# The first q load in float32 on SyncE's queue, and another emission order at the start

## The chip, the cores and the metric

The kernel runs on one NeuronCore of a Trainium2 chip. The metric is the device time of one execution in microseconds; times are medians over several executions. The core has five engines that each work through their own list of instructions strictly in order: TensorE (PE, matmuls into PSUM), VectorE (DVE), ScalarE (ACT), GpSimd (POOL) and SyncE (SP, which here only issues transfers). An instruction starts when those before it on its engine are issued and the results and buffers it needs are there. Transfers from HBM run on 16 shared DMA engines and are issued here from SyncE's list or from GpSimd's; a transfer that also converts float32 to float16 is issued from GpSimd's list in this kernel.

## The reference

First an attention with a feature map, with q, k and v of 8 batches, 8 heads, 576 positions and 64 channels, in float32:

```python
def phi(x):
    return np.where(x > 0, x, np.exp(x) - 1.0) + 1.0
q_p, k_p = (phi(q), phi(k))
kv = np.einsum('bhsd,bhse->bhde', k_p, v)
z = np.sum(k_p, axis=2)
num = np.einsum('bhsd,bhde->bhse', q_p, kv)
den = np.einsum('bhsd,bhd->bhs', q_p, z)[..., None] + 1e-06
return (num / den).astype(np.float32)
```

Its output is taken as x with 4608 rows (positions) and 512 columns. Then comes a mixture of 8 experts: `logits = x @ w_gate`, eight Sinkhorn rounds that scale the rows and columns of exp(logits) to a matrix P (4608 x 8), and

```python
for e in range(E):
    h = np.maximum(x @ w1[e], 0.0)
    ye = h @ w2[e]
    out += P[:, e:e + 1] * ye
```

with w1 of 512 x 1024 and w2 of 1024 x 512 for each expert.

## The kernel before, in words

**The attention.** It is done in 16 groups, n = 0 to 15, n = 2b + g for batch b and half g; a group is four heads. k0, q0, v0 below are the loads of group 0, and so on. A group takes these steps; what stands in square brackets is the group:

- three loads (line 376): k into a buffer `kin` in float32, q into `qin` and v into `vv` in float16, converted on the way. k of groups 0 and 1 is issued from SyncE, all else from GpSimd. There are three buffers of each kind.
- phi(k): exp on ScalarE (L387), add and max on VectorE (L391), min on VectorE (L395). phi(q) likewise: L450, L453, L457.
- kv[n]: 18 matmuls (L416) of phi(k) with v and with ones into the one PSUM buffer `kv_ps`; two copies (L335 or L337, `kvz`) take it to SBUF.
- qt[n]: nine transposes of phi(q) (L442) into `att`, and a copy of that to `qpT` (L335 or L337).
- den[n], two halves: a pair of matmuls each (L473 into `att`), then the logarithm on ScalarE (L486); after both halves exp of its negative (L491).
- num[n], two halves: a pair of matmuls each (L473 into `num_ps`, the same PSUM buffer as kv), then on VectorE the product with the reciprocal into xT (L501).

**What else runs in that time.** 46 matmuls on a constant tile (L593, `warm`) whose result nobody reads; the weights of expert 0 (L310, from GpSimd); the logits for two batches at a time (L518, L522); the first layer of expert 0 (L687, its relu L692 or L694) and its second layer (L935) for the first blocks of 512 positions, as soon as their part of xT is there; from the fifth block on a scheme with seven products in place of eight for a 2 x 2 block product (L813 for the first layer, L1053 for the second, with sums on VectorE in L985, L1024 and L851). The Sinkhorn rounds run on VectorE with one small matmul each (L559) and end before expert 1 needs P.

**What sets the order.** The kernel builds a list of tasks (`_Plan`), each with the engine or engines it can run on, durations and dependencies, and then emits them one by one. `_FRONT` is a long string that fixes the order of the first tasks: each word is a task number and a letter for the engine (p TensorE, a ScalarE, d VectorE, g GpSimd, s SyncE, m a landing, n none). So `66d` puts task 66 (the qpT copy of group 0) on VectorE and `66a` on ScalarE. As engines work in order, the string fixes what stands behind what. After the string a planner places the rest from the tasks' durations, and from the last block of expert 0 on TensorE's order is tied into a fixed chain. In the string 2p to 47p are the warm matmuls, 65p is qt[0], 58p kv[0], 67p and 69p den[0], 86p kv[1].

GpSimd issues at most eight of its loads ahead of landings (`p_sw`), and a load into a buffer waits for the last reader of what was in it.

Of the kernel before, what the change touches and what calls it, by code (L numbers as in the profile page):

```python
# [17 lines left out]
class _Plan:  # L18
# [121 lines left out]
    1n 108n 113n 595n 76s 77m 48s 49m 2p 3p 0g 4p 50g 51m 5p 6p 78g 79m 7p 8p 52g 53m 9p 80g 81m 10p 82a 83d 11p 118g  # L140
    119m 12p 13p 14p 15p 120g 121m 16p 84d 17p 54a 18p 146g 147m 19p 55d 20p 21p 22p 122g 123m 23p 56d 24p 61n 62a
    25p 26p 63d 27p 28p 29p 64d 30p 89n 109g 110m 90a 31p 32p 91d 65p 66d 57n 58p 148g 149m 92d 33p 59a 34p 85n 150g
    151m 35p 60a 36p 37p 67p 86p 68a 38p 125d 69p 39p 40p 87d 111g 112m 131n 124a 70a 41p 88d 71a 126d 93p 42p 94d
    74p 174g 175m 152a 75d 95p 43p 44p 96a 178g 179m 45p 72p 132a 73d 127n 97p 46p 47p 133d 128p 98a 134d 99a 129d
    135p 176g 177m 130d 202g 203m 153d 136a 100p 596p 101d 114g 115m 159n 597p 137p 154d 598p 138a 102p 161d 204g
    205m 160a 155n 103d 139p 599p 156p 140a 162d 141a 157d 163p 206g 207m 600p 164d 158a 602p 232g 233m 601d 165p
    142p 166a 181d 234g 235m 604p 606p 180a 143d 608p 603d 116g 117m 144p 609a 182d 167p 610p 607a 145d 183n 187n
    236g 237m 168a 612p 189d 188a 605d 184p 611d 260g 261m 169a 190d 614p 185d 191p 186a 632n 172p 192d 106g 107m
    618p 173d 193p 209d 170p 215n 208a 613a 615a 262g 263m 194a 616p 171d 216a 195p 210d 633p 290g 291m 217d 196a
    211n 218d 212p 197a 104g 105m 634d 219p 213d 635p 220d 214a 245n 238a 264g 265m 200p 239d 221p 637p 247d 636a  # L150
    201d 222a 639p 240d 246a 292g 293m 198p 223p 199d 617p 638a 248d 640a 241n 320g 321m 242p 224a 624d 225a 619p
    243d 318g 319m 244d 249p 267d 228p 250d 620p 273n 266a 346g 347m 229d 251p 621p 268d 252a 294g 295m 274a 226p
    297d 322g 323m 253p 641p 275d 254a 276d 643p 626a 269n 227d 255a 230p 642d 303n 305d 270p 231a 304a 644d 277p
    271d 622p 272a 278d 296a 258p 306d 279p 645p 324a 374g 375m 259d 331n 325d 647p 350g 351m 280a 298d 348g 349m
    646a 256p 623p 332a 257d 404g 405m 299n 281p 326d 665n 376g 377m 300p 282a 630d 283a 333d 307p 378g 379m 301d
    651p 308d 302a 628a 284p 309p 648a 285d 666p 310a 334d 286p 311p 667d 327n 668p 312a 353d 352a 670p 287d 335p
    669d 380a 359n 491g 492m 328p 336d 653p 329a 381d 408g 409m 330a 354d 313a 406g 407m 288p 382d 432g 433m 387n
    314p 289a 654p 360a 315d 337p 661d 316p 338a 672p 355n 317d 671a 339p 361d 673a 356p 362d 434g 435m 340a 553d
    649p 388a 495g 496m 554d 674p 357d 389d 358a 341a 363p 390d 676p 364d 417n 418a 344p 419d 365p 345d 650p 366a
    420d 342p 410a 367p 343d 383n 652p 368a 411d 384p 675a 412d 460g 461m 438a 391p 385d 436g 437m 677d 678p 445n  # L160
    386a 462g 463m 392d 369a 680p 503g 679d 493g 494m 659a 372p 447d 393p 373d 699p 394a 560d 681a 370p 395p 469s
    371d 413n 655p 396a 657d 397a 414p 439d 561d 421p 415a 464g 465m 440d 416a 682p 470s 497a 422d 400p 656p 401d
    446a 508n 423p 663d 698n 398p 424a 701p 441n 399d 425p 448d 442p 426a 471s 700d 500s 427a 449p 443d 501s 562d
    684p 502s 476n 450d 444a 563s 564m 509a 428p 451p 429d 685p 452a 498d 703p 477a 478d 555d 453p 430p 499d 556s
    557m 454a 683p 565s 566m 479d 692a 504n 402p 455a 431d 558s 559m 688p 510d 704a 511d 456p 403a 466a 689p 457d
    512p 467d 702a 458p 513d 705p 459d 480p 706a 468d 505p 481d 472n 707p 506a 581d 507a 582d 514p 473p 583d 515a
    584s 585m 690a 516p 474d 709p 517a 475d 686p 518a 735d 736d 482p 687p 710a 708d 696a 519p 737d 483a 711p 520d
    484p 738d 712a 713p 485a 574d 521p 739n 740p 486a 567d 522d 721p 714a 575d 694a 489p 576d 722p 490d 577s 578m
    719p 729d 568d 487p 717p 488d 718p 569d 551n 731d 570s 571m 742p 579s 580m 732d 778d 523p 743a 572s 573m 836d
    741a 720p 725a 733d 524a 552p 727a 525n 526d 744p 746p 745a 748p 747a 837d 588g 589n 592n 838d 527p 750p 779d  # L170
    749a 780d 734d 752p 781s 782m 751a 783s 784m 528d 754p 529d 753a 715p 839s 840m 755a 841s 842m 786p 716p 787a
    586s 587m 590g 591m 756d 530p 800p 785n 757d 792p 1009s 1010m 531d 788p 532d 762p 789a 723a 794p 793a 790p 760p
    791a 801a 796p 795d 802p 761a 758d 533p 806p 803a 797d 804p 807a 759d 766p 534d 798p 535d 808p 799a 810p 805a
    764p 767a 763a 844p 770p 845a 811d 765a 809d 768p 771d 536p 850p 537d 812p 769d 851a 772p 813a 894d 848p 814d
    773a 843n 858p 849a 895d 818p 815d 860p 816d 819a 846p 859a 817d 824p 847a 896d 861a 538d 864p 897s 898m 593g
    594m 820p 865a 825a 854p 868p 862p 866p 855d 863a 852p 869d 828p 867d 870p 821d 856p 829d 826p 857a 853d 539p
    902p 540d 822p 903a 541d 908p 823a 830p 871a 906p 831a 901n 904p 909a 952d 916p 905a 918p 872d 907a 876p 873d
    919a 912p 827d 877a 910p 917a 874d 924p 882p 953d 911d 922p 1001d 542p 878p 923a 954d 883d 955s 956m 920p 879a
    957s 958m 913d 926p 921a 875d 886p 925d 899s 900m 914p 543d 884p 927d 915a 1066s 1067m 887d 880p 544d 960p 888p
    961a 928p 889a 959n 966p 929a 964p 885d 967a 545p 934p 965a 930d 881a 970p 1002d 974p 935a 546d 976p 931d 975a  # L180
    962p 932d 978p 963a 980p 547d 977a 938p 981a 982p 940p 936p 933d 941a 971d 984p 937a 944p 1003d 979a 983d 942p
    945d 968p 985d 972p 969d 986p 973a 946p 943d 1522n 987a 1004d 548p 1012p 1000n 1011n 947d 1014p 1013a 549d 990p
    1015a 550d 1018p 1020p 1019a 1016p 774a 1022p 988p 777a 1023d 951a 631d 989p 1017a 1024p 726a 996d 1026p 625d
    1028p 1027a 1021d 991p 1029a 1005d 1025a 992p 1006d 629a 993p 1007d 1008d 1032p 1034p 627d 1033a 1030p 997d 1036p
    1031a 1069p 1037d 658a 994p 834d 1070a 1035d 1071p 939a 1038p 1072a 995p 1123s 1124m 998a 1039a 1075p 1068n 1525n
    1077p 999a 1040d 1073p 1076a 1044p 1041d 1042d 1046p 1045a 1043d 1049p 1048d 1047d 1079p 1050a 1054p 1074a 1080d
    835a 1057p 1056d 1052a 776d 1081p 1053g 1059d 1083p 1055d 1085p 1084a 1058d 1060p 660d 1086a 1082a 1089p 1062d
    1091p 1078d 1090a 1087p 695d 1093p 1088a 1061d 1126p 1094d 1128p 1127a 1092d 1063p 1129a 1095p 1065d 1125n 1132p
    1064d 1096a 1180s 1181m 1523g 1524m 1051g 1134p 664d 1133a 1130p 1097d 1101p 1098d 1103p 1099d 1102a 833a 1100d
    1106p 1104d 1136p 1105d 1107a 1111p 1109a 1137d 1131a 697d 1114p 662a 730d 1112d 693a 1138p 1110g 1113d 1140p  # L190
    691a 724d 1108g 1142p 1135d 1141a 1117p 1143a 892d 1116d 1139a 1146p 1115d 1148p 1147a 1118d 1144p 1149d 1150p
    1145a 1183p 1119d 1185p 775d 1184a 1120p 1151d 1186a 1152p 1122d 1182n 1189p 1121d 1153a 1237s 1238m 1191p 1190a
    1154d 1187p 1158p 1155d 1160p 1156d 1159a 1188a 1163p 1161d 1157d 1193p 1164a 1162d 1168p 1194d 1165g 1171p 1192d
    1526g 1527m 1170d 1195p 1169d 1197p 832d 1196a 1199p 891d 1198a 1174p 1173d 1200a 1203p 1176d 1205p 1175d 1204a
    1201p 1172d 1207p 1202a 1240p 1208d 1242p 1241a 1206d 1177p 1243a 1166a 1209p 1178d 1239n 1167g 1246p 1179d 1210a
    1294s 1295m 1248p 1211d 1244p 1215p 1212d 1217p 1213d 1216a 1247a 1220p 1218d 1214d 1250p 1223a 1219d 1225p 1245a
    1251d 1228p 728d 1226d 1224g 1227d 1252p 1229d 1254p 1253a 1528d 1256p 1255a 1231p 1249d 1257a 948d 1260p 1232d
# [22 lines left out]
def kernel(  # L220
# [27 lines left out]
    S_ = _Plan()  # L248
# [109 lines left out]
    def att(b, g):  # L358
        n = 2 * b + g
        pr = n - 100.0  # L360

        src = [[NJ * D, P], [4 * S * D, 2], [1, NJ * D]]
        gin, tin = {}, {}
        for nm, ten in (("k", k), ("q", q), ("v", v)):
            gr = gin[nm] = S_.grp(p_in[nm])
            sp = nm == "k" and b == 0

            def fn(_, gr=gr, nm=nm, ten=ten, sp=sp):
# [843 lines left out]
```

## Time and profile before

| | us |
|---|---|
| median of 3 runs | 962.06 (961.62 to 962.55) |
| the profiled execution | 961.32 |
| its span, first to last instruction | 959.4 |
| TensorE busy | 949.8 |
| VectorE busy | 786.9 |
| ScalarE busy | 575.9 |
| GpSimd busy | 145.3 |

The profile shows one execution. Busy times are sums over an engine's instructions without overlap; matmuls are pipelined and their ends are modelled, so TensorE's waits are better read from the starts of neighbouring matmul groups. In the rows that follow, a line of the order in time gives the start, the duration, engine, source line, operation, output and inputs, the shape, how many were merged (x18), and in square brackets the idle time before it with what ended it. A row of the waits gives who waited for whom, the total in us, how often, and the longest. A row of the table by stretches gives, for each engine, busy time and number of instructions in that stretch, then the granted TensorE clock, the share of the DMA engines, and GB/s. The granted clock was 0.999 of full speed.

### The profile page before, as it was taken

Reading aid. Unit: us, or ns where it says so; the run is one execution under the profiler, and the core shown is the slowest. Engines: PE = TensorE matmul, PEld = TensorE weight load, DVE = VectorE, ACT = ScalarE, POOL = GpSimd, SP = SyncE. Lnnn points to the kernel's source line nnn. Section 1 sums busy time; section 2 is a strip of 40 time slices with the busy share of each in tenths; the row PEclk is TensorE's granted clock in tenths of the full one; section 3 lists DMA queues with packets and bytes.
Section 4 is the critical chain, followed back from the end, with each engine's and each line's share of the span. In section 5 each row is a group of like instructions: output and inputs, shape, how many; then the busy total and the mean of one; then the engine's idle time right before and its main releaser. Section 6 shows DMA issues by size and latency. Waiting matters only on the chain.

```text
span 959.4 us, 21109 instructions
## 1 busy us (share of the span) xinstructions
PE 949.8 (99%) x8576; PEld 804.8 (84%) x8576; DVE 786.9 (82%) x1508; ACT 575.9 (60%) x1025; POOL 145.3 (15%) x209
## 2 busy tenths in 40 slices
PE   8999999999999999999999999999999999999998
PEld 4555578788888888888888888888888888888886
DVE  6999999898888888878887888878887888877775
ACT  6999665665555555555555555555555555555552
POOL 6432000011112111211112110111112111111110
PEclk9999999999999999999999999999999999999999
DMA  9997493044225422452227222272226322235554
GB/s 229 267 246 160 153 221 116 14 111 120 78 78 131 113 78 78 119 124 78 78 78 165 79 78 78 85 158 78 73 70 130 100 71 76 75 100 165 166 165 111
DMA packets 45821, 112.52 MB, mean 117 GB/s; under 512 B 4380, under 2 KB 25628, under 8 KB 45724
## 3 DMA queue, kind: packets, MB, share of 16 engines
q1 hardware_dynamic: 21340, 76.16, 23.9%
q0 software_dynamic: 23984, 34.48, 19.2%
q8 instruction: 67, 1.10, 0.5%
q10 hardware_dynamic: 400, 0.52, 0.2%
q14 instruction: 30, 0.25, 0.1%
HBM read 119.69 MB, written 17.69 MB: 143 GB/s over the span
## 4 chain that ended last, share of the span: by engine, by line
PE 93%; DVE 3%; ACT 1%; DMA 1%; issue 1%; POOL 0%; DVEq 0%; ACTq 0%; POOLq 0%
PE ye L1053 36%; PE hq L813 24%; PE R L813 12%; PE Zye L813 6%; PE Zye L1053 6%; PE ye L935 3%; PE hq L687 2%; DMA vv<-in_v_dram 1%; PE kv_ps L416 1%; PE att L473 1%; PE att L442 1%; PE num_ps L473 1%; DVE xT L501 1%; DVE h L694 0%; ACT rden L486 0%
## 5 line engine op out<-in xcount | busy, mean ns | idle before, releaser
L1084 DVE SCALAR_TENSOR_TENSOR acc<-ye,P_sb,acc 128x256 f32<-128x256 f32 x620 | 267.9, 479 | 119.6 <-PE ye L1053 118.5
L813 PEld LDWEIGHTS <-W 128*128 128x128 f16 x2144 | 209.7, 98 | 25.3 <-issue 0.2
L1053 PEld LDWEIGHTS <-S 128*128 128x128 f16 x1984 | 194.1, 98 | 22.9 <-issue 0.4
L1094 POOL TENSOR_TENSOR acc<-acc,st 128x256 f32<-128x256 f32 x124 | 88.6, 733 | 691.2 <-ACT st L1091 677.6
L1053 PE MATMUL ye<-T,S 128*128 128x256 f16 x1488 | 192.8, 273 | 0.2 <-DVE acc L1084 0.2
L813 PEld LDWEIGHTS <-w 128*128 128x128 f16 x1608 | 157.3, 98 | 19.2 <-issue 0.5
L1053 PEld LDWEIGHTS <-h 128*128 128x128 f16 x1584 | 155.0, 98 | 17.9
L848 ACT ACTIVATE h<-hq 128x512 f16<-128x512 f32 x134 | 80.0, 598 | 142.2 <-PE hq L813 137.3
L813 PE MATMUL hq<-xs,W 128*128 128x256 f16 x1008 | 151.2, 273 | 0.0
L813 PE MATMUL R<-xs,W 128*128 128x256 f16 x1008 | 151.2, 273 | 0.0
L813 PE MATMUL hq<-xs,w 128*128 128x256 f16 x1008 | 140.9, 273 | 0.3 <-DVE h L851 0.3
L845 ACT ACTIVATE h<-Zye 128x512 f16<-128x512 f32 x134 | 80.0, 597 | 39.3 <-PE Zye L813 39.3
L1091 ACT ACTIVATE st<-Zye,P_sb 128x256 f32<-128x256 f32 x124 | 52.5, 470 | 75.4 <-PE Zye L1053 75.4
L1024 DVE TENSOR_TENSOR S<-h 128x1024 f16<-128x1024 f16 x124 | 85.4, 689 | 12.2 <-ACT h L848 12.0
L835 ACT COPY s<-hq 128x512 f32<-128x512 f32 x126 | 73.5, 583 | 36.5 <-PE hq L813 36.2
L851 DVE CUSTOM_DVE_ANT_0 h<-R,s 128x512 f16<-128x512 f32 x126 | 86.6, 687 | 9.9 <-ACT s L835 9.4
L828 ACT COPY Zye<-hq 128x512 f32<-128x512 f32 x134 | 77.7, 580 | 27.5 <-PE hq L813 27.3
L851 DVE CUSTOM_DVE_ANT_0 h<-hq,s 128x512 f16<-128x512 f32 x126 | 86.7, 688 | 6.3 <-PE hq L813 6.2
L813 PE MATMUL Zye<-xs,w 128*128 128x256 f16 x504 | 75.6, 273 | 0.0
L842 ACT COPY s<-R 128x512 f32<-128x512 f32 x126 | 74.5, 591 | 0.0
L1053 PE MATMUL ye<-w,h 128*128 128x256 f16 x528 | 68.4, 273 | 0.0
L1053 PE MATMUL Zye<-w,h 128*128 128x256 f16 x528 | 68.4, 273 | 0.0
(116 smaller groups left out, 975.4 us busy)
## 6 DMA issues: line engine op xcount, KB each, us to landing
xs<-xd SPq DMA_DIRECT2D x63, 896.0 KB, 4.6
out_dram<-acc SPq DMA_DIRECT2D x67, 128.0 KB, 2.4
w<-in_moe_w_dram POOLq DMA_DIRECT2D x16, 512.0 KB, 8.6
kin<-in_k_dram POOLq DMA_DIRECT2D x14, 576.0 KB, 9.5
w<-in_moe_w_dram POOLq DMA_DIRECT2D x7, 1024.0 KB, 13.6
qin<-in_q_dram POOLq DMA_DIRECT2D x16, 288.0 KB, 8.2
vv<-in_v_dram POOLq DMA_DIRECT2D x16, 288.0 KB, 8.7
xd<-acc SPq DMA_DIRECT2D x5, 512.0 KB, 2.9
```

Source lines behind the costliest of these rows:

```text
L813: nc.tensor.matmul(dst[:, p, :], lhsT=lhs(p, c), rhs=rhs(c), start=(first and p == 0 and c == 0), stop=(c == 1), skip_group_check=True)
L828: nc.scalar.copy(out=Zt[1], in_=gX["tile"])
L835: nc.scalar.copy(out=gs2["tile"], in_=gX["tile"])
L842: nc.scalar.copy(out=gs5["tile"], in_=gR["tile"])
L845: nc.scalar.activation(out=hd(0, 0), in_=Zt[1], func=AF.Relu)
L848: nc.scalar.activation(out=hd(1, 0), in_=gX["tile"], func=AF.Relu)
L851: nc.vector._custom_dve(TENSOR_ADD_SAT, out=dst, in0=ps, in1=sb, s0=3.0e38, s1=0.0)
L1024: nc.vector.tensor_tensor(out=Sx[:, i], in0=a0, in1=a1, op=op)
L1053: nc.tensor.matmul(bank(g_)[:, s, :], lhsT=lhs(s, kk), rhs=rhs(kk), start=(new and s == 0 and kk == 0), stop=(kk == 3), skip_group_check=True)
L1084: nc.vector.scalar_tensor_tensor(out=dst(), in0=bank(g_)[:, s, :], scalar=P_sb[:, gg, e:e + 1], in1=dst(), op0=ALU.mult, op1=ALU.add)
L1091: nc.scalar.mul(out=gst["tile"], in_=bank(g_)[:, s, :], mul=P_sb[:, gg, e:e + 1])
L1094: nc.gpsimd.tensor_tensor(out=dst(), in0=dst(), in1=gst["tile"], op=ALU.add)
```

## The change

Three things change.

First, q of group 0 is loaded in float32, from SyncE's list, into a buffer of the k kind (`kin`). SyncE's list begins with k0, q0, k1 instead of k0, k1; GpSimd's list has one load less. The exp (L450) and add-and-max (L453) of group 0 read float32; the task's duration in the plan goes from 0.455 to 0.77.

Second, the plan's earliest landing time for a load from GpSimd goes from 4.0 to 5.2.

Third, `_FRONT` is another string: 1510 words instead of 1582. GpSimd's loads then begin v0, q1, v1, k2, q2, v2, k3, two pieces of w1, q3, v3 instead of q0, q1, v0, v1, k2, q2, k3, v2, two pieces of w1, q3, v3. TensorE's list begins, with w for warm matmuls:

- before: 31 w, qt[0], kv[0], 5 w, den[0], kv[1], w, den[0], 3 w, qt[1], w, num[0], den[1], 3 w, num[0], den[1], 2 w, kv[2], qt[2], num[1], 2 half-jobs of L687, den[2], one more, num[1], den[2], one more, kv[3]
- after: 27 w, qt[0], w, kv[0], w, den[0], kv[1], den[0], 3 w, qt[1], w, num[0], 3 w, den[1], num[0], 2 w, den[1], 2 w, kv[2], 2 w, qt[2], w, num[1], 3 w, den[2], one half-job of L687, num[1], two more, den[2], kv[3]

The choice between VectorE and ScalarE for copies, relus and scalings changes with the string. The lines of the changed kernel stand one to three lower than before.

```diff
 _FRONT = """
-    1n 108n 113n 595n 76s 77m 48s 49m 2p 3p 0g 4p 50g 51m 5p 6p 78g 79m 7p 8p 52g 53m 9p 80g 81m 10p 82a 83d 11p 118g
-    119m 12p 13p 14p 15p 120g 121m 16p 84d 17p 54a 18p 146g 147m 19p 55d 20p 21p 22p 122g 123m 23p 56d 24p 61n 62a
...
+    1n 108n 113n 595n 48s 49m 50s 51m 2p 3p 76s 77m 0g 4p 52g 53m 5p 6p 78g 79m 7p 8p 80g 81m 9p 10p 55d 11p 12p 13p
+    14p 15p 16p 17p 61n 54a 118g 119m 62a 63d 18p 19p 120g 121m 20p 21p 22p 23p 122g 123m 64d 24p 25p 26p 146g 147m
...
         for nm, ten in (("k", k), ("q", q), ("v", v)):
-            gr = gin[nm] = S_.grp(p_in[nm])
-            sp = nm == "k" and b == 0
-
-            def fn(_, gr=gr, nm=nm, ten=ten, sp=sp):
+            wide = nm == "k" or n == 0 and nm == "q"
+            gr = gin[nm] = S_.grp(p_in["k" if wide else nm])
+            sp = wide and b == 0
+
+            def fn(_, gr=gr, nm=nm, ten=ten, sp=sp, wide=wide):
...
-                elif nm == "k":
+                elif wide:
                     dst = gr["tile"] = fp.tile([P, 2, NJ, D], FP32, tag="kin", name="kin", bufs=NK)
...
-            tin[nm] = fadd(("dma", 1.47 if nm == "k" else 1.42), lambda _: None, deps=[ti], use=[gr, *gsw], prio=pr, lat=2.2,
-                           after=0.0 if sp else 4.0)
+            tin[nm] = fadd(("dma", 1.47 if wide else 1.42), lambda _: None, deps=[ti], use=[gr, *gsw], prio=pr, lat=2.2,
+                           after=0.0 if sp else 5.2)
...
-        t3 = fadd(("dve", 0.455), f_qm, deps=[t0], use=[gin["q"], gtq], prio=pr)
+        t3 = fadd(("dve", 0.455 if n else 0.77), f_qm, deps=[t0], use=[gin["q"], gtq], prio=pr)
```

## The prediction

> **What bounds the kernel now.** I read the table of stretches first, then the waits and the order in time at the start.
>
> ```profile
> core 0: us, PE busy (x) PEld busy (x) DVE busy (x) ACT busy (x) POOL busy (x), PEclk, DMA share, GB/s
> 0.00:10.00 10.00, 8.67 (x31) 3.45 (x31) 5.66 (x11) 4.77 (x4) 8.29 (x17) 1.00 0.87 199
> 10.00:20.00 10.00, 8.20 (x82) 4.94 (x81) 6.73 (x11) 7.73 (x10) 4.84 (x7) 1.00 1.14 268
> 20.00:30.00 10.00, 9.28 (x87) 5.50 (x86) 9.23 (x17) 8.74 (x11) 5.77 (x9) 1.00 1.16 247
> 30.00:60.00 30.00, 29.56 (x277) 17.30 (x276) 28.67 (x48) 28.26 (x38) 13.34 (x19) 1.00 1.15 259
> 60.00:120.00 60.00, 59.42 (x543) 34.34 (x544) 57.20 (x104) 49.86 (x73) 10.31 (x17) 1.00 0.70 173
> ...
> 200.00:900.00 700.00, 699.75 (x6411) 627.00 (x6410) 567.32 (x1094) 398.51 (x749) 93.39 (x131) 1.00 0.35 99
> ```
>
> From 200 to 900 us TensorE is never free (699.75 of 700), and the change touches nothing there. Before, TensorE is still the fullest engine, but VectorE and ScalarE are nearly as full (28.67 and 28.26 of 30), and the DMA engines are full until 60 us (shares above 1). Both kernels give TensorE the same 8576 matmuls, the 46 warm ones of L593 among them. So **the time can change only by TensorE's waits**, and nearly all of those lie before 180 us.
>
> ```profile
> PE att L442 <- DVE tq L457: 1.0, 2, 0.7
> PE att L473 <- DVE qpT L337: 0.5, 1, 0.5
> PE att L442 <- ACT rden L486: 0.4, 1, 0.4
> ```
>
> These rows (first 30 us) are too small, because the modelled ends of matmuls overlap. I count from start to start instead: four 512-column matmuls take 0.865 us where nothing waits, a pair of L473 0.245, a kv group 0.85, the nine transposes 0.505, a warm one 0.216. What is above that is wait. By this count TensorE waits 4.1 us from the end of the 31st warm matmul (10.0) to the fourth kv group (25.61), 4.0 us from there to 118 us in some 22 pieces of 0.1 to 0.5, and 0.7 us between 118 and 180. More than these 8.8 us is not to be had.
>
> ```profile
> 4.81 1.16 ACT L387 ACTIVATE ek<-kin 128x1152 f16<-128x1152 f32 x1 [2.79 <-DMA kin<-in_k_dram]
> 6.26 1.16 ACT L387 ACTIVATE ek<-kin 128x1152 f16<-128x1152 f32 x1 [0.29 <-DMA kin<-in_k_dram]
> 8.83 1.16 ACT L450 ACTIVATE eq<-qin 128x1152 f16<-128x1152 f16 x1 [1.40 <-DMA qin<-in_q_dram]
> 10.39 1.16 ACT L450 ACTIVATE eq<-qin 128x1152 f16<-128x1152 f16 x1 [0.40 <-DMA qin<-in_q_dram]
> 11.75 0.92 PE L416 MATMUL kv_ps<-vv,t 64*128 64x192 f16 x18 [0.23 <-DMA vv<-in_v_dram]
> 14.68 0.76 DVE L391 TENSOR_SCALAR t<-kin 128x1152 f16<-128x1152 f32 x1 [1.71 <-DMA kin<-in_k_dram]
> ```
>
> These are landings: k0 4.81, k1 6.26 (SyncE's queue), then by GpSimd's queue q0 8.83, q1 10.39, v0 11.75 and, two further, k2 14.68. So v1 landed at about 13.2: one load each 1.45 us, whichever queue, since the engines are full.
>
> **The change, part by part.**
>
> *Landings.* On SyncE's queue q0 becomes the second of three loads: it lands at 6.26 where k1 did, 2.6 us earlier, and k1 third, at 7.7. GpSimd's queue first moves packets at 5.4 us, as the stretch from 5 to 6 us shows for the two queues:
>
> ```profile
> q1 hardware_dynamic: 114, 0.23, 64.0%
> q0 software_dynamic: 59, 0.07, 58.0%
> ```
>
> (58% of that microsecond; none before it.) So v0 shares the engines with k1; I take k1 at 7.9 and v0, now fourth, at 9.9. q1 follows at 11.4, v1 at 13.2, k2 at 14.6. A full pipe is not made faster: from v1 on everything lands when it did. v2 moves ahead of k3 and lands at about 17.5 instead of 19.0.
>
> *GpSimd.* One issue less, 0.73 us. It waits 0.5 to 1.0 us for a free place before nearly each issue after 9 us, so this is worth nothing. Its fourth issue, k2, now needs k0's buffer, since q0 took the third: it goes from 5.16 to 6.0 (k0's last reader ends at 5.97), with q2, v2, k3 and a piece of w behind it. From issue to first packet is 3.2 us (2.17 to 5.4), so k2's packets are there at 9.2; v0, q1 and v1 keep the engines busy until about 11.2. Hidden, unless that reader is 2 us later. k3 waits for q0's readers (7.4) and is hidden likewise.
>
> *VectorE.* L453 for q0 takes the f32 time (0.76, as L391) instead of 0.46: +0.30 us, beside VectorE's own wait for loads. The new order also moves small work: over the program VectorE has 8 instructions fewer, among them five L903 at 0.49 and two kvz copies at 0.42, ScalarE 8 more. That is about 3.5 us less on VectorE, all before 190 us.
>
> *TensorE at the start.* I follow the new order with these durations. 27 warm matmuls instead of 31 end at 9.14. q0: ScalarE 6.26 to 7.42, L457 to 8.24, so the transposes run at 9.14 without a wait (before: 10.84). kv[0] at 9.9; qpT on ScalarE 9.85 to 10.97, kvz to 11.33, den[0] at 11.52 (0.55 waited). kv[1] stands next and needs v1: **13.2, waiting 1.43**. Then den, three warm, qt[1] at 15.3 (0.35, behind L486), num[0] and den[1] to 17.25, second num[0] at 17.56 (0.3, L501), kv[2] at 19.1 (0.17, L501), kv[3] at 24.6 (0.45, v3, which lands as before). With small ones 3.5 us of wait to kv[3], against 4.1. kv[3] comes 1.0 us earlier, with one half-job of L687 (0.433) still owed: **-0.5 us**. The early q itself is lost at kv[1]: TensorE stands there with 17 warm matmuls (3.7 us) behind the wait instead of before it. Bounds: +2.9 (two loads late, below) and -2.0 (half of the old waits).
>
> *25 to 118 us.* Here the order counts. I added up what stands ahead of the first den of a group in each engine's list, at the pitches above. Before den[5], [7], [13] TensorE has 33.1, 46.5, 81.3 us in the old order and 34.9, 48.2, 83.6 in the new; VectorE has 28.9, 41.8, 77.0 and 28.9, 41.9, 76.7; ScalarE 29.3, 41.9, 75.7 and 28.2, 42.5, 76.3. So for the same VectorE work TensorE has 1.6 to 2.6 us more to do meanwhile. The old pieces are 0.1 to 0.5 us each, so those made by queues should go. Those made by direct handing on (num, L501, num; den, L486, qt) need some 1.0 us of other work between: the new order mostly has 1.11 or 1.97, the old mostly 1.11. I take half of 4.0: **-2.0 us**; bounds 0 and -4.0, and +1.5 if the new pieces are as many and longer. At den[3] alone the new order is tighter (ScalarE 2.2 us behind TensorE's list, 2.8 before).
>
> *118 to 180 us.* At the Sinkhorn matmuls (L559) the same count has VectorE 5.9 to 7.2 us ahead at the five tight ones of the eight in the old order, and 6.6 to 8.1 in the new; the three others have 6.9 or more in both. So nothing speaks for new waits, but the old 0.7 us has other makers too: **0**; bounds -0.7 and +1.0. After that the order is a fixed chain and the same: 0.
>
> *Sum.* -2.5 us. The profiled execution took 961.32 us (span 959.4 and 1.92 around it): 958.8. It lay 0.74 below the median of three, so against that median **959.6 us**.
>
> **Rule and row.** The warm matmuls pitch 0.427 us until 5.2 us and 0.213 after; TensorE's longest wait in the front was 0.84 us, and no slow matmul is seen later. My replay has it idle for 2.0 of the 2.45 us before 13.2. [...]
>
> **The rivals.**
>
> 1. *No gain.* The early lead ends at kv[1] anyway, and the later waits come back in other places, because they are handing-on and not queues. For it: num to num and den to den gaps of 1.11 us are still common. Against: the leads above. Time: 962.06 - 0.5 = 961.5.
> 2. *Slower: loads late at kv[1].* The third load on SyncE's queue and v0 compete from 5.4 us, and GpSimd stands at k2. If v1, v2 and v3 land two places late (2.9 us), TensorE waits for each: no L687 work stands ahead of den[2], and the warm matmuls are behind the wait. -0.5 + 2.9 and no later gain: 964.5. It decides from v1 later than about 15.6. Against: the landing rows are evenly 1.45 apart on either queue.
> 3. *Slower: ScalarE at den[3].* 17.6 us of its work stand ahead of that den; from 4.81 they end at 22.4 plus its idle time, and my replay has den[3] at 27.0. So 4.4 us of idle are free and each further one is a wait. It idled 3.9 us between 4.81 and 20 before (five waits, all shown as for loads or TensorE); I forecast 3.2. If the wait at kv[1] and new ones behind it make that 7.2: -0.5 + 2.8 and no later gain, 964.4. Against: it decides only from 6.8.
> [...]
>
> **How the numbers follow.** Forecast 0.45, rival 1 0.28, rival 2 0.15, rival 3 0.07, rival 4 0.05. 0.2% (1.9 us) is about what a measurement of this kernel can tell from no change: faster is below 960.14, slower above 963.98. Faster holds the forecast, 0.45; same rivals 1 and 4, 0.33; slower 2 and 3, 0.22. The forecast's own range is 957.0 to 960.1: all bounds but the last microsecond. The range goes to 965.0 to take in 1, 4 and the middle of 2 and 3, and leaves some 0.05 below and 0.12 above.
>
> **What would show it.** Right: first transposes at about 9.1 us, kv[1] at 13.2 and waiting for vv, kv[2] at 19.1, kv[3] at 24.6; first L559 matmul at about 118.7 (before 121.19); waits between 25 and 118 near 2 us; the last matmul some 2.5 us earlier. Wrong: q0's first reader later than 6.5 (queue shared otherwise), kv[1] after 14 (rival 2), slow matmuls after 12 us (rival 4), or the same 4 us of pieces from 25 to 118 (rival 1).

## The result, and the profile after

The changed kernel takes **959.13 us** (median; 958.77 to 960.15) beside 962.06 (961.62 to 962.83) of the kernel before on the same chip. The ratio is 0.9969, 95% interval 0.9958 to 0.9981: 0.3% faster, and the forecast was 959.6. The profiled execution took 959.15 us with a span of 957.3, 2.1 us below the span before. By the medians the gain is 2.9 us: the profiled execution of the kernel before, with 961.32 us, was quicker than all seven that the median is taken of, so 0.8 us of the gain lies outside what the two traces can show. All times in the table are from the start of the span; the fourth kv group is the fourth of group order, n = 3.

| | before | after | forecast |
|---|---|---|---|
| first transposes, qt[0] | 10.84 | 9.53 | 9.14 |
| kv[0] | 11.75 | 11.07 | 9.9 |
| kv[1] | 14.03 | 13.32 | 13.2 |
| kv[2] | 20.33 | 19.16 | 19.1 |
| kv[3] | 25.61 | 24.54 | 24.6 |
| first Sinkhorn matmul (L559, after L556) | 121.19 | 120.14 | 118.7 |
| last of the eight | 176.16 | 175.40 | - |
| end of the span | 959.4 | 957.3 | - |

First the table of stretches of the changed kernel:

```profile
core 0: us, PE busy (x) PEld busy (x) DVE busy (x) ACT busy (x) POOL busy (x), PEclk, DMA share, GB/s
0.00:10.00 10.00, 8.67 (x36) 3.72 (x37) 4.76 (x10) 4.04 (x4) 7.57 (x16) 1.00 0.88 240
10.00:20.00 10.00, 8.27 (x92) 4.87 (x89) 8.48 (x15) 9.09 (x11) 4.55 (x7) 1.00 1.14 267
20.00:30.00 10.00, 9.35 (x78) 5.45 (x77) 8.97 (x15) 8.83 (x11) 5.80 (x9) 1.00 1.16 236
30.00:60.00 30.00, 29.60 (x276) 17.20 (x275) 26.43 (x44) 26.71 (x38) 11.89 (x17) 1.00 1.17 267
60.00:120.00 60.00, 59.30 (x552) 34.59 (x548) 57.90 (x107) 50.37 (x73) 11.40 (x17) 1.00 0.69 170
...
200.00:900.00 700.00, 700.00 (x6414) 626.03 (x6413) 564.90 (x1089) 401.79 (x754) 92.75 (x130) 1.00 0.34 99
```

What changed most is not TensorE but the two engines behind it: from 30 to 60 us VectorE is busy for 26.43 us instead of 28.67 and ScalarE for 26.71 instead of 28.26, while TensorE's 29.60 is as before. They have more slack there now. Part of it is work that stands elsewhere: VectorE is busy for 8.48 us instead of 6.73 from 10 to 20 us, and for 57.90 instead of 57.20 from 60 to 120. The slack does not show as busier TensorE.

The chain of the start, in order of time on ScalarE and TensorE:

```profile
4.59 1.16 ACT L384 ACTIVATE ek<-kin 128x1152 f16<-128x1152 f32 x1 [2.57 <-DMA kin<-in_k_dram]
6.10 1.16 ACT L447 ACTIVATE eq<-kin 128x1152 f16<-128x1152 f32 x1 [0.34 <-DMA kin<-in_q_dram]
9.57 1.16 ACT L384 ACTIVATE ek<-kin 128x1152 f16<-128x1152 f32 x1 [2.31 <-DMA kin<-in_k_dram]
11.07 0.92 PE L413 MATMUL kv_ps<-vv,t 64*128 64x192 f16 x18 [0.65 <-DVE t L392]
13.32 0.92 PE L413 MATMUL kv_ps<-vv,t 64*128 64x192 f16 x18
```

q0 is read at 6.10, where the second k load was read before. But the third load, k1, is not read at 7.9 but at 9.57. VectorE's list has L388 of that k ahead of L392 of group 0, so kv[0] waits for VectorE and not for a load. How k1 came late stands in the DMA queues' rows of two later microseconds (q1 is SyncE's queue, q0 GpSimd's; packets, MB, share of 16 engines). From 7 to 8 us:

```profile
q0 software_dynamic: 164, 0.19, 109.5%
q1 hardware_dynamic: 28, 0.03, 10.7%
```

and from 9 to 10 us:

```profile
q0 software_dynamic: 192, 0.20, 119.8%
q1 hardware_dynamic: 2, 0.00, 0.8%
```

From 6 to 7 us SyncE's queue still moved 140 packets. Once GpSimd's is running, the last 35 of k1 take over 2 us more, the last two of them after 9.

**Where the 2.1 us of span come from.** I compare how far each kernel has got in its own list of work at common marks, with the matmul pitches of the prediction. To kv[3]: 25.61 against 24.54, of which one half-job of L687 (0.433) is still owed, so -0.64. From kv[3] to the first Sinkhorn matmul 95.58 against 95.60, with that half-job paid back: -0.41. From the first to the last Sinkhorn matmul 54.97 against 55.26, but the new list has 0.87 us more TensorE work there (164.25 against 163.38 us of listed work up to the last one): -0.58. From there to the end 783.24 against 781.9, with those 0.87 no longer owed: -0.47. The sum is -2.1, in four parts of about equal size. The border between the first two is not firm: in the second trace of the changed kernel kv[3] stands at 24.93, 0.28 of it waiting for v3, and the four parts are -0.25, -0.66, -0.57 and -0.47. The start differs from one execution to the next; from the first Sinkhorn matmul on the two traces differ by 0.01.

### The profile page after: what moved, and what is told of

Read it like the earlier page. It is cut to its first block, busy times and chain, and to the rows that moved or that the text cites. A ratio compares the mean times of both kernels' runs of the same rounds, so it can differ in the third digit from the quotient of the medians.

```text
span 957.3 us, 21101 instructions
## 1 busy us (share of the span) xinstructions
PE 948.3 (99%) x8576; PEld 803.3 (84%) x8576; DVE 781.5 (82%) x1500; ACT 579.7 (61%) x1033; POOL 144.0 (15%) x208
## 3 DMA queue, kind: packets, MB, share of 16 engines
q0 software_dynamic: 23712, 34.19, 19.1%
## 4 chain that ended last, share of the span: by engine, by line
PE 90%; DVE 4%; ACT 3%; issue 1%; DMA 1%; SPq 0%; DVEq 0%; ACTq 0%
PE ye L1050 36%; PE hq L810 24%; PE R L810 12%; PE Zye L810 6%; PE Zye L1050 6%; PE ye L932 2%; PE hq L684 2%; ACT rden L483 1%; DVE xT L498 1%; DMA kin<-in_k_dram 1%; ACT eq L447 1%; ACT rden L488 1%; DVE t L392 0%; DVE tq L454 0%; ACT ek L384 0%
```

## The experiments

Each group of runs shares its runs of the kernel before (962.36, 961.8 and 961.51 us in the three groups), so ratios are what compares across groups. A number and letter in the order string is one task and the engine that it is given to. The changed kernel, run again in the first group, came to 959.19 us, 0.9970 (0.9958 to 0.9981).

> The changed kernel itself, as the measure for the three others on the same chip: 959.1, ratio 0.9969.

### Is it q's load or the order?

The early float32 q in the old order (changed kernel, old string, q0 put between the two k loads of SyncE's queue):

```diff
-    1n 108n 113n 595n 48s 49m 50s 51m 2p 3p 76s 77m 0g 4p 52g 53m ...
+    1n 108n 113n 595n 76s 77m 50s 51m 48s 49m 2p 3p 0g 4p 5p 6p 78g 79m ...
```

> The old emission order, with only the first q changed: float32, SyncE's queue, second of its three loads (k1, q0, k0). Theory A (the order carries the gain; the early q is taken back at the second kv group, which waits for v1 at about 13.1 us either way): as before, 962.1, between 961.5 and 962.8; q0's reader starts at about 6.1 us, k0's, now third on SyncE's queue, at about 9.5 instead of 6.3, and the second kv group at about 13.5 to 14. Theory B (the early q carries it): 960.0 to 960.7.

And the new order with q0's load as before (kernel before, new string, q0 from GpSimd's queue):

```diff
-    1n 108n 113n 595n 48s 49m 50s 51m 2p 3p 76s 77m 0g 4p 52g 53m ...
+    1n 108n 113n 595n 48s 49m 2p 3p 76s 77m 0g 4p 50g 51m 52g 53m ...
```

> The new emission order, with the first q as before: float16, GpSimd's queue, as the first of its loads. Theory A (the order carries the gain): 959.4, between 958.9 and 960.0, with the first transposes at about 10.8 us instead of 9.5 but the second kv group at about 13.4 and the fourth at about 24.5, as in the changed kernel. Theory B (the early q carries it): 961.0 to 962.0, with the first four kv groups 1 us or more later.

Measured: q alone 963.4 us, 1.0016 (1.0006 to 1.0026); the order alone 959.57 us, 0.9974 (0.9965 to 0.9983). **The order makes the gain; the early q by itself brings none, and costs a little.** The string also gives work to other engines: the run with the order alone has 1500 instructions on VectorE and 1033 on ScalarE, as the changed kernel, and the run with q alone 1508 and 1025, as the kernel before. No run separates the order from these choices, so "the order" means both here. ScalarE of the run with q alone shows why the early q brings nothing:

```profile
4.90 1.16 ACT L386 ACTIVATE ek<-kin 128x1152 f16<-128x1152 f32 x1 [2.88 <-DMA kin<-in_k_dram]
8.03 1.16 ACT L386 ACTIVATE ek<-kin 128x1152 f16<-128x1152 f32 x1 [1.97 <-DMA kin<-in_k_dram]
9.10 1.15 ACT L449 ACTIVATE eq<-kin 128x1152 f16<-128x1152 f32 x1
```

Second in the queue, q0 has no wait for a load in front of it any more (the third row has none), but in this list its exponential stands behind that of the last k, which now comes at 8.03 instead of 6.26. It starts at 9.10, later than the 8.83 of before, and kv[3] is at 26.45 instead of 25.61. This trace is of the quickest of the eleven executions (961.62 us). Where the others lose more is not shown; in the four of 963.74, 963.8, 965.63 and 966.18 us the mean granted clock was 0.998 or 0.997, and in the seven others, with 1.000 or 0.999, the median is 963.02. What the changed kernel has beyond the order alone (0.9970 beside 0.9974) can't be told from nothing.

### Does the lead at the start last?

The changed kernel with VectorE's L392 of group 0 ahead of L388 of group 1, so that kv[0] no longer waits behind the late k1:

```diff
-    83d 27p 28p 65p 56d 109g 110m ...
+    56d 83d 27p 28p 65p 109g 110m ...
```

> The changed kernel with two of VectorE's instructions exchanged: the min of group 0 (L392) stands ahead of the add-and-max of group 1 (L388), which waits for k1 until 9.57 us. The first kv group should start at about 10.3 instead of 11.07. Theory A (v1's landing sets the second kv group): 959.1, no more than 0.3 away. Rival (the late k1 costs the end what it costs the first kv group): 958.3 to 958.6.

Measured 958.69 us, 0.9969 (0.9958 to 0.9979), no change beside 0.9970. kv[0] comes at 9.79 and kv[1] at 12.04, 1.28 us ahead of the changed kernel, and the fourth kv group gives it back:

```profile
24.53 0.92 PE L411 MATMUL kv_ps<-vv,t 64*128 64x192 f16 x18 [1.14 <-DMA vv<-in_v_dram]
```

It starts where it did (24.54), and v3 holds it. Not all of the lead need be the edit's: in this execution the 27 warm matmuls ended at 8.97 us instead of 9.53, and k1 was read at 7.92 instead of 9.57. To see whether the landing of v3 is the limit, q2's load was replaced by a fill, first on GpSimd:

```diff
+                if n == 2 and nm == "q":
+                    nc.gpsimd.memset(dst, 0.1)
+                    return
```

> The kernel with the exchanged pair (e3_m0_first), and the load of q2 left out: GpSimd fills its buffer with a constant instead, so group 2's output is wrong. That takes one load of 1.45 us out of the stream ahead of v3. Theory A (v3's landing sets the fourth kv group): that group at about 23.2 to 23.6 instead of 24.53, and 957.7, between 957.3 and 958.2. Rival (something else holds it): 958.7, as with the load.

Measured 958.74 us, 0.9971 (0.9960 to 0.9983). That decided nothing, because the lead to be lost was not there: kv[0] was at 10.79. VectorE was held up beside the fill. GpSimd and VectorE in order of time:

```profile
6.93 1.08 POOL L372 MEMSET qin<- 128x1152 f16 x1
```

```profile
6.24 2.38 DVE L451 TENSOR_SCALAR tq<-kin 128x1152 f16<-128x1152 f32 x1 [0.74 <-DMA kin<-in_q_dram]
```

VectorE's add-and-max for q0 took 2.38 us instead of 0.76 (6.10 us, changed kernel) beside that fill. But the late kv[0] is mostly not the fill's: the 27 warm matmuls lasted to 9.98 us in this execution, the transposes followed at once, and kv[0] stands 0.81 behind them, as in the run before (0.82). By itself the fill would have cost less: VectorE's L393 for kv[0] was done at 10.16. The same with the fill on VectorE (`nc.vector.memset`):

> As the run that replaced q's load for group 2 by a fill, but filled by VectorE in place of GpSimd, since under GpSimd's fill VectorE's L451 took 2.38 us in place of 0.76. The output is not the reference's: group 2's q is a constant. Theory A, v3's landing set kv[3] where L392 comes early (1.14 us of wait there): v3 lands about 0.7 us earlier with 0.29 MB less to load, kv[3] at 23.6 to 24.0 us, and about 0.6 us off the time, 958.0 us. Rival, TensorE or VectorE holds kv[3] at 24.4 anyway or the lead is lost later: 958.7 us.

Measured 958.55 us, 0.9969 (0.9958 to 0.9981). By the medians that is no change, as the rival has it. At the fourth kv group itself the theory of v3 holds by the trace: the wait is gone,

```profile
23.55 0.92 PE L414 MATMUL kv_ps<-vv,t 64*128 64x192 f16 x18
```

0.98 us earlier than with q2's load. In the two traces the lead lasts: the first Sinkhorn matmul at 118.78 (119.84 with the load), the last at 174.08 (175.14), the span 956.3 (957.1). But these traces do not stand for their kernels alike: this one is of the quickest of six executions (958.08, median 958.55), the other of one above its median (958.9, median 958.69). So v3 is shown to hold the fourth kv group where L392 comes first; that its wait costs the whole kernel time is not shown.

### Does TensorE's own work set the start?

The changed kernel without the last 19 warm matmuls, whose output nothing reads:

```diff
-        twa = add(("pe", ...), f_warm, deps=[twa], ...)
+        twa = add(("pe", ...), f_warm if i < 27 else (lambda _: None), deps=[twa], ...)
```

> The changed kernel without the 19 warm matmuls that stand behind the first transposes (27 stay). Nothing of the computation is left out, since nobody reads them. Theory A (up to the fourth kv group the landing of v3 sets the pace, and the warm matmuls only fill TensorE's waits): 959.1, between 958.6 and 959.6, with the fourth kv group still at about 24.5. Rival (TensorE's work and its waits add up, as the prediction counted it): 19 x 0.216 = 4.1 us less, 955.0. Rival (the clock falls back when TensorE idles): matmuls of 0.427 us pitch after 12 us, and 961 to 963.

Measured 959.34 us, 0.9979 (0.9970 to 0.9988). 4.1 us less for TensorE before kv[3], and kv[3] only 0.46 us earlier (24.08). By the start-to-start count its gaps between 10 and 20 us grow from 2.6 to about 5 us. So the work of TensorE does not set the start: it is paced by loads and by results of VectorE and ScalarE, and the late warm matmuls fill its waits. One thing more goes with them. The mean granted clock is 1.000 or 0.999 in all 13 executions of the changed kernel, but 0.998 to 0.994 in 8 of the 11 without them, and the time goes with it: 958.14 to 958.67 us in the three with 0.999 or 1.000, 959.05 to 959.57 in the five with 0.998, 959.93 and 960.19 with 0.996, 961.37 with 0.994. The profiled execution (958.67) is one of the three, so no trace shows where the clock fell. The rival of the clock is therefore right in part (the clock was lower; that idle time of TensorE is what lowers it was not shown), and the median says little of the start alone. Both edits together:

> The changed kernel with VectorE's L392 of group 0 ahead of L388 of group 1, and without the last 19 warm matmuls, whose output nothing reads. Theory A, the loads and VectorE pace the start: at best both small leads together (0.4 us by the span without the warm matmuls, 0.2 with L392 moved), 958.3 to 958.8 us. Rival, TensorE's list paces the start once L392 is early: 19 x 0.216 us comes off, 955 us. A third, slow matmuls in the stretches now idle (a granted clock under 1.0, 128x512 matmuls over 0.3 us): 960 us or more.

Measured 958.87 us, 0.9973 (0.9962 to 0.9984), kv[3] at 24.00, again behind v3:

```profile
24.00 0.92 PE L411 MATMUL kv_ps<-vv,t 64*128 64x192 f16 x18 [0.71 <-DMA vv<-in_v_dram]
```

Not the 955 us of the rival. Nor are there slow matmuls in this trace: the mean of the 128x512 group of L932 (L930 here) is 379 ns in both kernels, the mean granted clock is 1.0, and TensorE's longest wait from 5 to 30 us is 1.1 us. But the trace is again of a quick execution (958.42). Of the seven, three had a mean granted clock of 0.998 or 0.996, and they took 958.87, 959.45 and 959.58 us; the four others took 958.28 to 958.98.

### Is it VectorE's queue that the new order relieves?

VectorE's L392 (L395 before) is left out in groups 4 to 13, ten times 0.76 us, in the new order and in the old:

```diff
-        (..., f_m, ...)
+        (..., (lambda _: None) if 4 <= n <= 13 else f_m, ...)
```

> The changed kernel without the min (L392) of phi(k) in groups 4 to 13: ten VectorE instructions of 0.68 us pitch, 6.8 us of VectorE's work between 25 and 95 us, are left out, and phi(k) of these groups is wrong by that. Theory H (TensorE's pieces of wait between 25 and 118 us come from handing results on, not from VectorE being behind): 958.5 to 959.3. Theory Q (they come from VectorE's queue): 1.5 to 2.5 us less, 956.6 to 957.6.

> The kernel before without the same ten instructions (its L395, groups 4 to 13; phi(k) of these groups is wrong by that). Theory H: 961.5 to 962.2. Theory Q: VectorE stood closer to TensorE in this order, so it gains at least as much as the changed kernel does: 959.5 to 960.5.

In the new order 958.69 us, 0.9972 (0.9961 to 0.9982), no change beside 0.9970. In the old order 960.09 us, **0.9982 (0.9973 to 0.9991): 1.7 us faster**. So VectorE's load cost the old order time and costs the new one none that can be measured (the intervals would hide some 1 us). The edit also shortens the chain from k's landing to the kv group by one step in these ten groups, so by itself the 1.7 us could be either; where the time was won tells more. The stretches of the old order with less VectorE work:

```profile
30.00:60.00 30.00, 29.34 (x279) 17.27 (x277) 25.87 (x43) 28.56 (x39) 13.18 (x20) 1.00 1.17 270
60.00:120.00 60.00, 59.84 (x546) 34.38 (x544) 54.30 (x100) 49.64 (x73) 10.63 (x17) 1.00 0.69 169
```

VectorE has 25.87 of 30 here, near the changed kernel's 26.43. Of the 1.2 us of span (958.2 against 959.4), 0.27 are there by kv[3], which lies ahead of the edit; 0.30 come between kv[3] and the first Sinkhorn matmul (120.62), **0.62 between the first and the last** (54.35 us instead of 54.97), and nothing after. The last piece lies behind all ten left-out instructions, so it is VectorE's queue and not a shorter chain: two waits of the old order, 0.33 us at 148.1 and 0.27 at 157.3, are not in this trace. In the two traces VectorE's queue cost the old order more behind 120 us than in the attention groups.

### Which half of the order?

The kernel before, with the entries that its list has ahead of the first Sinkhorn matmul put in the new order and the rest left; and the reverse. In words of the list (703 entries are ahead):

```diff
-old = first 703 entries, rest
+front new = first 703 in the new list's order, rest as it was
+back new  = first 703 as they were, rest in the new list's order
```

> The kernel before (its loads and its code), with the work that the old list has ahead of the first L559 matmul (703 of 1582 entries) put in the new list's order, and everything from that matmul on left in the old order. Theory F, all of the gain comes from the start and the attention groups: as the order alone, 959.4 to 959.9 us. Theory S, about half is made before the first L559 matmul (by the milestones 1.05 of 2.1 us) and half by the later list: 960.7 to 961.2 us.

> The kernel before, with the old order up to the first L559 matmul (703 entries) and the new list's order for all that is left. Theory F: no change, 961.8 to 962.4 us. Theory S: half the gain, 960.8 to 961.3 us. If this and the kernel with the new front each gain by themselves, their gains should add up to that of the order alone (0.26%).

Measured: the new front 961.77 us, 1.0003 (0.9994 to 1.0012); the new back 960.25 us, 0.9987 (0.9978 to 0.9996). Neither theory: the front brings nothing, the back half, and together (0.9974) they bring more than the sum, at the edge of what the intervals can tell. The front does bring the first Sinkhorn matmul 0.72 us earlier, to 120.47, as the whole new order does (120.38); the second is then 0.57 later than before. TensorE with the new front, in order of time:

```profile
120.47 0.28 PE L557 MATMUL R<-gs,ones_t 128*128 128x8 f32 x2
...
126.65 0.39 PE L557 MATMUL R<-gs,ones_t 128*128 128x8 f32 x2 [0.79 <-DVE gs L552]
```

It waits for a reduction on VectorE, which ran there at

```profile
119.58 0.45 DVE L552 TENSOR_REDUCE gs<-wt 128x8 f32<-128x288 f32 x1
119.95 0.68 DVE L997 TENSOR_TENSOR xT<-w,xT 128x1024 f16<-128x1024 f16 x1
...
126.14 0.45 DVE L552 TENSOR_REDUCE gs<-wt 128x8 f32<-128x288 f32 x1
```

and in the kernel before at

```profile
120.16 0.45 DVE L554 TENSOR_REDUCE gs<-wt 128x8 f32<-128x288 f32 x1
...
125.47 0.45 DVE L554 TENSOR_REDUCE gs<-wt 128x8 f32<-128x288 f32 x1
```

6.56 us from one to the next instead of 5.31. The cut lets three pieces of VectorE work (0.68 and two of 0.42) fall between them that the old list has ahead of the first, and VectorE is without a gap there. So the cut made its own cost, and the two halves can't be priced this way. What it does show: around 120 us VectorE and not TensorE sets the time, and 0.7 us of lead of TensorE are worth nothing if VectorE's list is 0.7 us longer.

Further on the two traces can be compared wait by wait. The old order has TensorE waiting for 0.33 us at 148.1 and for 0.41 at 246.5. The new front still has both (0.31 at 148.6, 0.41 at 246.8); the new back and the changed kernel have neither. So these two go with the later part of the list. The eight instructions that VectorE has fewer belong there too: the new front has 1508 on VectorE and 1025 on ScalarE, the new back 1500 and 1033. The second wait has a cause in sight, in the kernel before:

```profile
244.24 2.54 POOL L1094 TENSOR_TENSOR acc<-acc,st 128x256 f32<-128x256 f32 x3 [10.73 <-ACT st L1091]
244.39 1.12 DVE L985 TENSOR_TENSOR W<-W,w 128x1024 f16<-128x1024 f16 x1
246.95 1.03 PE L1053 MATMUL ye<-T,S 128*128 128x256 f16 x8 [0.25 <-DVE acc L1084]
```

VectorE's sum takes 1.12 us instead of 0.68 beside GpSimd's, what stands behind it on VectorE comes late, and TensorE waits for that. All four traces with the old list there have TensorE wait for `acc` at that place (0.25 or 0.26 us by the modelled ends). In the changed kernel no such sum takes over 0.82 us, and TensorE has no wait there.

## Why the prediction was right, and where it was not

- **Only TensorE's waits can change: right.** TensorE's matmuls are 8576 in both, and from 200 to 900 us it is busy 700.00 of 700. VectorE has 1500 instructions instead of 1508 and ScalarE 1033 instead of 1025, as counted; but not all before 190 us, up to where VectorE has one instruction and 1.0 us of busy time less.
- **Landings: one right, one wrong, one not seen.** q0 at 6.26 came at 6.10. k1 at 7.9 came at 9.57: the term was the author's estimate, with GpSimd's traffic as a fair share of the engines, and here 35 packets of k1 were still to come at 7 us, two of them after 9 (in four other kernels' traces the third load was read at 7.84 to 8.15, as forecast). GpSimd's queue moved no packet before 6 us and 33 from 6 to 7, where the forecast had it begin at 5.4. v1 at 13.2 was too late: kv[1] ran at 12.04 without waiting for v in the run with L392 first. One slip of naming, in the prediction and in the list of the change: SyncE's list began with k1, k0 before, so what is called k0 there is the k load of group 1. No number hangs on it.
- **GpSimd: right.** k2 was issued at 6.06 (6.0 forecast), and nothing waited for it.
- **TensorE at the start, -0.5: right in size (-0.64, and -0.25 in the second trace), wrong in its steps.** The 27 warm matmuls lasted to 9.53 instead of 9.14. kv[0] was not at 9.9 but at 11.07, 0.65 of it waiting for L392 behind the late k1; kv[1], at 13.32 for a forecast of 13.2, did not wait for v1 at all. Two errors met, and that the term came out is luck: the wait that was forecast at kv[1] stood at kv[0]. That an earlier q is lost again further on was right, though at kv[3] and v3, as the traces with L392 moved and with q2's load taken away show.
- **25 to 118 us, -2.0: the engine right, the term mis-sized.** It measured -0.41 (-0.66 in the second trace). TensorE's pieces of wait in that stretch still add up to 3.9 us after 4.0, which the prediction had named as the sign of rival 1. Less VectorE work did free 1.7 us in the old order and none in the new, so the new list does relieve VectorE. But most of these pieces did not go. That they are handing-on from engine to engine, as rival 1 had it, fits the new order, where less VectorE work won nothing; it was not tried piece by piece.
- **118 to 180 us, 0, and later 0: wrong.** They brought -0.58 and -0.47. The prediction saw VectorE 5.9 to 7.2 us ahead by its list at the Sinkhorn matmuls and called that enough. The run with less VectorE work in the old order won 0.62 us there, and the run with the new front had TensorE waiting for VectorE there for 0.79. Most of the last 0.47 is the piece at 246.1 us of the kernel before, where four matmuls of L813 take 0.85 us from start to start instead of 0.44, and which goes with the later part of the list. VectorE's sum of 1.12 us beside GpSimd's is in front of it in the kernel before; no run moved that sum alone.
- **The sum** held (-2.5 against -2.1 of span and -2.9 by the medians) by luck: the stretch that was priced 1.6 us too high lies beside two that were priced at nothing and brought 1.05. In those VectorE was the engine waited for, as the prediction had it for the stretch before.
- **Rivals.** Rival 2 fell: kv[1] came at 13.32, before its 15.6. Rival 3 fell with it: from kv[3] to the first Sinkhorn matmul no time was lost. Rival 4, slow matmuls after 12 us, did not occur: the granted clock is 1.00 in every stretch, and 0.999 or 1.000 in every execution of the changed kernel. No run shows what would bring such a stretch on, nor what it would cost, though the range to 965.0 takes it in. It is no empty rival: without the late warm matmuls the clock did fall, to 0.998 to 0.994 in 8 of 11 executions, which took 959.05 to 961.37 us beside 958.14 to 958.67 for the three others. Rival 1 was right on the pieces from 25 to 118 us and wrong on the time.

## What to carry to other kernels

Here three engines were nearly full (28.26 to 29.56 us from 30 to 60 us), and the earlier load bought nothing by itself (1.0016): look at what stands in each engine's list ahead of its first reader, and at which later load gives the lead back. To see whether an engine's queue costs time, leave some of its work out in both orders; that told more here than counting gaps, because work left out before 95 us won time behind 120 us (0.62 us). Matmuls whose result nobody reads can look like mere filling, and yet here the mean granted clock was 0.999 or 1.000 in all 13 executions of the changed kernel and lower in 8 of 11 without the late ones: compare the granted clock of all executions, not only of the profiled one. A list of work cut in two and joined anew made its own wait at the joint here (0.79 us), so read that joint before trusting the halves.

## What the runs showed of the hardware

- **The tail of a load.** The third load on SyncE's queue was first read at 9.57 and 9.58 us in the two profiles of the changed kernel and at 7.92, 8.03, 8.15 and 7.84 in four others, with the three issues at 0.74, 1.24 or 1.25, and 1.74 us in slow and quick ones alike. In the four quick ones its packets ended before 8 us. In the two profiles of the changed kernel, the run without the late warm matmuls, the run with less VectorE work in the new order and the run with GpSimd's fill the queue still moved 5, 10, 5, 11 and 5 packets from 8 to 9 us. The first four of these have the changed kernel's own list at the start; the quick ones are the old order with q alone and three of the four with L392 moved first. The traces show shares far from even (28 packets to 164 from 7 to 8 us, then 2 to 192 from 9 to 10), but not what sets them. From 7 to 8 us a quick run looks the same (27 packets to 166, with the fill on VectorE). Nothing that the traces show before 8 us explains the tail, and it stays open.
- **A fill on GpSimd and an add-and-max on VectorE at the same time.** 2.38 us for the latter instead of 0.76, with the 1.08 us fill inside it. By the rows VectorE had started first (6.24 and 6.93 us), and it lost 1.62 us, more than the fill lasted. With the fill on VectorE the same add-and-max took 0.76, from 6.21 us on. It is one execution, and why the instruction took longer is not shown.
- **The first warm matmuls.** 27 of them from 1.33 us on lasted to 8.79 in one run (less VectorE work, new order) and to 9.98 in another (GpSimd's fill), the same instructions. That 1.2 us of spread is as large as most leads at the start that were tried here.
- **The late warm matmuls and the clock.** With them every execution of the changed kernel had a mean granted clock of 0.999 or 1.000; without them 11 of 18 had 0.994 to 0.998. (The run with q alone has them all, and four of its eleven had 0.997 or 0.998.) In the two profiled executions without them, both with 1.00, TensorE's longest waits from 5 to 30 us were 1.0 and 1.1 us. How long they were where the clock fell is not shown.
